# Loading filter rows in long transfers, and moving the reordering of columns into the moving read of the row-tiled matmuls

## The chip, the cores and the metric

One core of a Trainium2 chip. The metric is the device time of one execution in microseconds (us). Only runs of the fast state are compared; the slow ones are named. Ratios are computed as the mean time of one kernel's fast runs over the mean of the other kernel's fast runs of the same rounds, so they aren't quite the ratio of the medians that the text quotes. Intervals are at 95%.

Terms: PE is TensorE's matmuls and PEld its weight loads, DVE is VectorE, ACT is ScalarE, SP is SyncE, which issues most transfers. SBUF is the core's memory for data, PSUM the one that matmuls write. A matmul's stationary operand (the weights) is loaded first; then its moving operand is read (back to back, g1's matmuls of 128 columns start 56 ns apart, f2's of 256 columns 109 ns). An eviction copies a result from PSUM to SBUF. A row-tiled matmul here uses 64 of the 128 rows; two of them start 3 to 4 ns apart and run side by side.

## The reference, cut to what matters

```python
# x: (1, 2048, 512) bf16;  w_r, w_i: (2048, 257) bf16
def _A_ref(x, w_r, w_i):                       # spectral filter
    X = jnp.fft.rfft2(x.astype(jnp.float32), axes=(-2, -1))
    X = X * (w_r + 1j * w_i)
    return jnp.fft.irfft2(X, s=(S, D), axes=(-2, -1)).astype(jnp.bfloat16)

h  = x + _A_ref(_layernorm(x), w_r, w_i)
h2 = h + _B_ref(_layernorm(h), w1, b1, w2, b2) # MLP over the 2048 rows, F = 1376
```

The kernel computes both Fourier transforms as matmuls. Only the part around the product `X * W` matters here. The 257 columns of W are used as column 0 apart and 256 columns, which the transform delivers in two halves, by parity.

## The kernel before

The kernel builds a list of operations and orders them for each engine with a model of its own. These are the parts that the change touches (`...` marks cuts).

```python
add("W", [NP, NG, 2, LW], bf, rw)       # 128 x 32 rows g x (real, imaginary) x 257
add("CS", [NP, 16, 2, 2, NP], bf, rd)   # [group G][parity y][c][j]

# filter rows: three chunks (units 0, 1-3, 4-7), each row of 257 its own run of 514 B
for w, dram in ((0, A_w_r), (1, A_w_i)):
    for comp in range(2):
        d = W[comp::4, g0:g0 + ng, w, :]                     # "plus" rows, ascending
        lst.append(dma(..., d, bass.AP(dram.tensor, g0 * LW, [[64 * LW, 32], [LW, ng], [1, LW]]), ...))
        d = W[2 + comp::4, h0:h0 + nh, w, :]                 # "minus" rows, descending
        lst.append(dma(..., d, bass.AP(dram.tensor, (64 - h0) * LW, [[64 * LW, 32], [-LW, nh], [1, LW]]), ...))
        ...

# f2: matmuls into one bank, evicted to CS in the order (parity, c, j)
dst = CS[:, G, :, :, :].rearrange("p y c j -> p (y c j)")
cs_ops[G] = act(f"cs_{G}", dst, lambda bank: ps[:, bank, :], ACT.Copy, ...)

# x: row-tiled matmuls, 64 rows each, two at once, eight for each unit u
mm(f"x_{G}_{c}{r}", lambda bank, r=r, i=i: ps[:, bank + r, i * 256:i * 256 + 256],
   M[rows, ..., c, :], CS[rows, G, :, c, :], ...)

# V: product with the filter, VectorE, 2048 columns for each unit
wt = W[:, g0 + h * ng:g0 + h * ng + ng, :, :]
win = bass.AP(wt.tensor, wt.offset + 1, [list(wt.ap[0]), [LW, 2 * ng], [1, 2], [2, NP]])
eng.tensor_tensor(vout, s, win, ALU.mult)

# g1: V is the stationary operand
mm(f"g1_{g}_{par}{w}", ..., V[:, g, w, par * NP:par * NP + NP], R[:, ..., w, :], ...)
```

A unit u goes through f2 (TensorE), CS (ACT), x (TensorE), V (VectorE), g1 (TensorE), PQ (ACT). There are eight units. After all of them come g2 and g3, the second normalisation, and the MLP.

## Time and profile before

| | before |
|---|---|
| time | 134.44 us, median of 3 runs (134.16 to 134.53); a fourth run came later |
| V stage on VectorE | 22.0 to 39.9 us |
| first g2 matmul (all units done) | 41.32 us |
| row-tiled group of eight, start to the next group's start | 0.54 us |
| W's 514 B packets, first start to last end | 12.1 to 29.9 us |

The chain of waits by line, from the page of the kernel before. It follows the work back from the last instruction, each step to what released it.

```profile
PE ps L527 50%; DVE V L735 13%; DVE H L795 7%; DMA X<-in_A_x_dram 5%; ACT Y L545 5%; DVE TT L786 4%; DVE TT L788 4%; DVE HH L800 4%; ACT rs L545 1%; ACT FS L545 1%; DVE st L649 1%; SPq L517 1%; DVE OUT L825 1%; ACT PQ L545 0%; PE ps L617 0%
```

V holds 13% of it. No transfer but that of X is in it.

The timeline of VectorE around the V stage, kernel before. Columns: start in us, length in us, engine, line, operation, out<-in, shape, count, idle time before and what ended it.

```profile
22.02 17.88 DVE L735 TENSOR_TENSOR V<-ps,W 128x1024 bf16<-128x1024 f32 x10 [0.93 <-PE ps L527]
```

The ten V products run in one stretch without a gap between them.

The same view of TensorE, cut to the first and the last units. A line is a run of equal matmuls; `CS,EM` is a row-tiled group, `EM,V` is g1, `EM,Y` is f2, `EM,PQ` is g2.

```profile
21.27 0.61 PE L527 MATMUL ps<-CS,EM 64*128 64x256 bf16 x8
21.81 0.61 PE L527 MATMUL ps<-EM,Y 128*128 128x256 bf16 x4
...
34.66 0.61 PE L527 MATMUL ps<-CS,EM 64*128 64x256 bf16 x8
35.21 0.39 PE L527 MATMUL ps<-EM,Y 128*128 128x256 bf16 x2
35.44 0.72 PE L527 MATMUL ps<-EM,V 128*128 128x128 bf16 x10
36.29 0.61 PE L527 MATMUL ps<-CS,EM 64*128 64x256 bf16 x8
36.83 0.51 PE L527 MATMUL ps<-EM,V 128*128 128x128 bf16 x6
37.69 1.07 PE L527 MATMUL ps<-EM,V 128*128 128x128 bf16 x16 [0.35 <-DVE V L735]
38.91 0.61 PE L527 MATMUL ps<-EM,V 128*128 128x128 bf16 x8 [0.15 <-DVE V L735]
...
41.32 0.94 PE L527 MATMUL ps<-EM,PQ 128*128 128x256 bf16 x7 [0.69 <-ACT PQ L545]
```

Lengths overlap (a matmul of 256 columns takes about 270 ns, but the next starts about 109 ns after it), so read the starts: a row-tiled group takes 21.81 - 21.27 = 0.54 us. TensorE is nearly as full as VectorE here: busy 17.15 of the 17.90 us from 22.0 to 39.9.

The groups by form (busy us, mean ns of one | idle before), kernel before:

```profile
L735 DVE TENSOR_TENSOR V<-ps,W 128x2048 bf16<-128x2048 f32 x6 | 13.3, 2282 | 0.0
L527 PE MATMUL ps<-EM,V 128*128 128x128 bf16 x128 | 9.2, 219 | 0.5 <-DVE V L735 0.5
L545 ACT ACTIVATE CS<-ps 128x512 bf16<-128x512 f32 x15 | 8.3, 608 | 2.1 <-PE ps L527 2.1
L527 PEld LDWEIGHTS ps<-EM,V 128*128 128x128 bf16 x128 | 7.5, 98 | 2.3 <-issue 1.4 <-DVE V L735 0.8
L527 PE MATMUL ps<-CS,EM 64*128 64x256 bf16 x64 | 4.9, 272 | 0.2
L527 PE MATMUL ps<-EM,Y 128*128 128x256 bf16 x64 | 8.7, 273 | 0.4 <-ACT Y L545 0.4
L527 PE MATMUL ps<-EM,PQ 128*128 128x256 bf16 x64 | 9.0, 273 | 0.7 <-ACT PQ L545 0.7
```

And the transfers of the page, kernel before:

```profile
DMA packets 16648, 22.16 MB, mean 167 GB/s; under 512 B 2720, under 2 KB 12960, under 8 KB 16128
```

### The profile page before, as it was taken

The numbers are of one execution on the slowest core, as the hardware profiler recorded it, in microseconds if no ns is written. First come the engines' busy times: TensorE is split into PE (matmuls) and PEld (weight loads), VectorE is DVE, ScalarE is ACT, GpSimd is POOL, SyncE is SP. The second block draws the span as 40 slices with busy tenths as digits, with TensorE's granted clock in tenths as the row PEclk, the third lists the DMA queues.
The fourth block names the chain that finished last, engine by engine and source line by source line (L and its number), as shares of the span: only waits on it lengthen the run. The fifth ranks groups of instructions, "written<-read, shape, count | busy, mean of one in ns | idle before, by whom it ended". The sixth has DMA issues, their size and how long they took to land.

```text
span 133.0 us, 2023 instructions
## 1 busy us (share of the span) xinstructions
PE 125.4 (94%) x786; PEld 75.3 (57%) x786; DVE 69.2 (52%) x127; ACT 63.4 (48%) x146; POOL 12.2 (9%) x33
## 2 busy tenths in 40 slices
PE   6999989999987979999999999999999999999990
PEld 2356756878656726644434444456666666666660
DVE  0379975999990999999970000000242332423322
ACT  4569976878966999986679322222000000000000
POOL 0288830000300000000000000000000000000000
PEclk9999999999999999999999999999999999999999
DMA  3999698999999999992000000000111112111121
GB/s 94 335 370 382 178 276 229 304 317 264 411 430 430 398 411 409 419 281 89 0 0 0 0 0 0 5 0 0 39 39 64 55 39 81 42 59 59 39 79 39
DMA packets 16648, 22.16 MB, mean 167 GB/s; under 512 B 2720, under 2 KB 12960, under 8 KB 16128
## 3 DMA queue, kind: packets, MB, share of 16 engines
q1 hardware_dynamic: 16352, 21.52, 47.3%
q10 hardware_dynamic: 288, 0.52, 1.3%
q8 instruction: 6, 0.10, 0.3%
q14 instruction: 2, 0.02, 0.0%
HBM read 19.95 MB, written 2.10 MB: 166 GB/s over the span
## 4 chain that ended last, share of the span: by engine, by line
PE 51%; DVE 33%; ACT 8%; DMA 5%; issue 1%; SPq 1%; DVEq 0%; ACTq 0%
PE ps L527 50%; DVE V L735 13%; DVE H L795 7%; DMA X<-in_A_x_dram 5%; ACT Y L545 5%; DVE TT L786 4%; DVE TT L788 4%; DVE HH L800 4%; ACT rs L545 1%; ACT FS L545 1%; DVE st L649 1%; SPq L517 1%; DVE OUT L825 1%; ACT PQ L545 0%; PE ps L617 0%
## 5 line engine op out<-in xcount | busy, mean ns | idle before, releaser
L527 PE MATMUL ps<-HH,W 128*128 128x512 bf16 (+1 forms) x176 | 40.7, 379 | 1.2 <-DVE HH L800 0.9
L527 PE MATMUL ps<-GT,W 128*128 128x512 bf16 (+1 forms) x176 | 38.2, 379 | 0.0
L825 DVE SCALAR_TENSOR_TENSOR OUT<-ps,B2f,H 128x512 bf16<-128x512 f32 x16 | 12.0, 750 | 48.7 <-PE ps L527 48.7
L527 PEld LDWEIGHTS ps<-GT,W 128*128 128x128 bf16 (+1 forms) x176 | 25.4, 144 | 12.7
L527 PEld LDWEIGHTS ps<-HH,W 128*128 128x128 bf16 (+1 forms) x176 | 17.2, 100 | 21.2 <-DVE HH L800 1.9
L735 DVE TENSOR_TENSOR V<-ps,W 128x2048 bf16<-128x2048 f32 (+1 forms) x10 | 17.9, 1856 | 0.9 <-PE ps L527 0.9
L545 ACT ACTIVATE GT<-ps,B1f 128x512 bf16<-128x512 f32 (+1 forms) x11 | 7.1, 688 | 14.6 <-PE ps L527 14.6
L545 ACT ACTIVATE JK<-H,nm 128x512 bf16<-128x512 bf16 x16 | 11.6, 724 | 3.0 <-DVE H L795 2.9
L617 PE MATMUL ps<-ZT 128*128 128x512 bf16 x34 | 11.3, 479 | 1.3 <-DVE ZT L613 1.2
L649 DVE BATCH_NORM_STATS2 st<-X 128x6 f32<-128x512 bf16 x14 | 9.3, 668 | 5.3 <-DMA X<-in_A_x_dram 5.3
L795 DVE TENSOR_TENSOR H<-ps,TT 128x512 bf16<-128x512 f32 x16 | 10.9, 681 | 0.0
L545 ACT ACTIVATE PQ<-ps 128x512 bf16<-128x512 f32 x16 | 8.9, 603 | 3.5 <-PE ps L527 3.2
L545 ACT ACTIVATE EO<-ps 128x512 bf16<-128x512 f32 x16 | 9.3, 599 | 0.9 <-PE ps L527 0.9
L527 PE MATMUL ps<-EM,V 128*128 128x128 bf16 x128 | 9.2, 219 | 0.5 <-DVE V L735 0.5
L527 PE MATMUL ps<-EM,PQ 128*128 128x256 bf16 x64 | 9.0, 273 | 0.7 <-ACT PQ L545 0.7
L545 ACT ACTIVATE CS<-ps 128x512 bf16<-128x512 f32 x15 | 8.3, 608 | 2.1 <-PE ps L527 2.1
L527 PE MATMUL ps<-EM,Y 128*128 128x256 bf16 x64 | 8.7, 273 | 0.4 <-ACT Y L545 0.4
L527 PEld LDWEIGHTS ps<-EM,V 128*128 128x128 bf16 x128 | 7.5, 98 | 2.3 <-issue 1.4
L629 POOL TENSOR_SCALAR FS<-FP,rs 128x256 bf16<-128x256 bf16 x9 | 8.3, 935 | 1.3 <-ACT rs L545 1.3
L527 PE MATMUL ps<-FS,X 128*128 128x256 bf16 x64 | 8.3, 273 | 0.1
L786 DVE TENSOR_TENSOR TT<-ps,X 128x256 f32<-128x256 f32 x16 | 6.7, 416 | 3.3 <-PE ps L527 3.3
L527 PEld LDWEIGHTS ps<-EM,PQ 128*128 128x128 bf16 x64 | 6.2, 98 | 2.9 <-ACT PQ L545 0.9
(36 smaller groups left out, 80.3 us busy)
## 6 DMA issues: line engine op xcount, KB each, us to landing
W<-in_B_w_dram SPq DMA_DIRECT2D x4, 1376.0 KB, 11.0
W<-in_B_w_dram SPq DMA_DIRECT2D x10, 512.0 KB, 17.6
out_dram<-OUT SPq DMA_DIRECT2D x16, 128.0 KB, 1.7
W<-in_A_w_r_dram SPq DMA_DIRECT2D x4, 257.0 KB, 4.3
W<-in_A_w_i_dram SPq DMA_DIRECT2D x4, 257.0 KB, 5.0
X<-in_A_x_dram SPq DMA_DIRECT2D x4, 256.0 KB, 5.8
X<-in_A_x_dram SPq DMA_DIRECT2D x2, 512.0 KB, 7.7
W<-in_A_w_r_dram SPq DMA_DIRECT2D x4, 192.8 KB, 3.5
```

What stands on the lines that cost most here:

```text
L517: return eng.dma_start(dst, src)
L527: return K.op(name, "pe", lambda eng, bank: eng.matmul(outf(bank), lhsT, rhs, start=start, stop=stop), ins=ins or [lhsT, rhs], occ=occ, la ...
L545: return eng.activation(dst, s, func, **kw)
L617: return K.op(name, "pe", lambda eng, bank: eng.matmul(ps[:, bank, :], ZT[:, 0:NP], ZT[:, :], start=True, stop=True), ins=[ZT[:, :]], occ= ...
L629: dve(f"fs{i}", lambda eng, bank: eng.tensor_scalar(FS[:, i, :, :], FP[:, i, :, :], rs, None, op0=ALU.mult), [FP[:, i, :, :], rs], [FS[:, ...
L649: dve(f"st_{i}", lambda eng, bank, i=i, x=x: eng.bn_stats(ST[:, i, 0:6], x), [x], [ST[:, i, 0:6]], 512, prio=25)
L735: return eng.tensor_tensor(vout, s, win, ALU.mult)
L786: dve(f"tl_{s2}", lambda eng, bank, tt=tt, xl=xl: eng.tensor_tensor(tt[:, 0, :], ps[:, bank, 256:512], xl, ALU.add), [xl], [tt[:, 0, :]], ...
L788: dve(f"th_{s2}", lambda eng, bank, tt=tt, xh=xh: eng.tensor_tensor(tt[:, 1, :], xh, ps[:, bank, 256:512], ALU.subtract), [xh], [tt[:, 1, ...
L795: return eng.tensor_tensor(hs.rearrange("p (h d) -> p h d", h=2), e, tt[:, :, :], ALU.add)
L800: dve(f"hh_{s2}", lambda eng, bank, s2=s2, hs=hs: eng.tensor_scalar(HH[:, s2, :], hs, NM[:, s2:s2 + 1], R2[:, s2:s2 + 1], op0=ALU.add, op1 ...
L825: dve(f"fin{s2}", lambda eng, bank, dst=dst, bia=bia, hs=hs: eng.scalar_tensor_tensor(dst, ps[:, bank, :], bia, hs, op0=ALU.add, op1=ALU.add),
```

## The change

The intent is to make the filter's transfers cheaper. The plus rows ascend in memory, so with W laid out component first, `[NP, 2, NG, LW]`, the rows of one partition are one long run (2 to 8 KB instead of 514 B), and one transfer can write both component partitions. But then the V product's read of W would be a pattern of component, row, parity and column: four dimensions, where its operands in the trace have three (W's is 128 x 2 x 8 for a product of 2048 columns). Whether four would do was not tried. So the columns are put back in natural order before V: the row-tiled matmuls read CS alternately from both parities. V then reads W at unit stride, and g1 reads its weights in steps of two.

```diff
-    return 4 * (k2 * 2 + s) + 2 * sign + comp
+    return 4 * (k2 * 2 + s) + 2 * comp + sign
...
-    add("W", [NP, NG, 2, LW], bf, rw)
+    add("W", [NP, 2, NG, LW], bf, rw)
...
+            d = W[0:NP:2, w, g0:g0 + ng, :].rearrange("p g l -> p (g l)")
+            lst.append(dma(f"ld_wp{ch}_{w}", d, bass.AP(dram.tensor, g0 * LW, [[64 * LW, 32], [0, 2], [1, ng * LW]]), ...))
             for comp in range(2):
-                d = W[comp::4, g0:g0 + ng, w, :]
-                lst.append(dma(f"ld_wp{ch}_{w}{comp}", d, bass.AP(dram.tensor, g0 * LW, [[64 * LW, 32], [LW, ng], [1, LW]]), ...))
...              (minus rows: as before, other partitions; the loads of row 0 are joined too: 20 transfers, not 28)
-    M[rows, ...], CS[rows, G, :, c, :], ...
+    M[rows, ...], CS[rows, G, :, c, :].rearrange("p y j -> p j y"), ...
...
-    win = bass.AP(wt.tensor, wt.offset + 1, [list(wt.ap[0]), [LW, 2 * ng], [1, 2], [2, NP]])
+    win = bass.AP(wt.tensor, wt.offset + 1, [list(wt.ap[0]), [LW, ng], [NG * LW, 2], [1, 256]])
...
-    V[:, g, w, par * NP:par * NP + NP], R[...]
+    V[:, g, w, par::2], R[...]
```

More of the change, by code (lines that the diff above doesn't have):

```diff
@@ L578, in build_kernel @@
         for w, dram in ((0, A_w_r), (1, A_w_i)):
+            d = W[0:NP:2, w, g0:g0 + ng, :].rearrange("p g l -> p (g l)")
+            lst.append(dma(f"ld_wp{ch}_{w}", d, bass.AP(dram.tensor, g0 * LW, [[64 * LW, 32], [0, 2], [1, ng * LW]]),
+                           64 * ng * 514, prio=42 - ch, group=f"w{ch}"))
+            h0, nh = (g0, ng) if g0 else (1, ng - 1)
             for comp in range(2):
-                d = W[comp::4, g0:g0 + ng, w, :]
-                lst.append(dma(f"ld_wp{ch}_{w}{comp}", d, bass.AP(dram.tensor, g0 * LW, [[64 * LW, 32], [LW, ng], [1, LW]]),
-                               32 * ng * 514, prio=42 - ch, group=f"w{ch}", rate=300.0))
-                h0, nh = (g0, ng) if g0 else (1, ng - 1)
-                d = W[2 + comp::4, h0:h0 + nh, w, :]
+                d = W[1 + 2 * comp::4, w, h0:h0 + nh, :]
                 lst.append(dma(f"ld_wm{ch}_{w}{comp}", d, bass.AP(dram.tensor, (64 - h0) * LW, [[64 * LW, 32], [-LW, nh], [1, LW]]),
                                32 * nh * 514, prio=42 - ch, group=f"w{ch}", rate=300.0))
-                if g0 == 0:
-                    d = W[2 + comp::4, 0, w, :]
-                    lst.append(dma(f"ld_wz{ch}_{w}{comp}", d, bass.AP(dram.tensor, 32 * LW, [[64 * LW, 32], [1, LW]]),
-                                   32 * 514, prio=42 - ch, group=f"w{ch}", rate=300.0))
+            if g0 == 0:
+                d = W[1:NP:2, w, 0, :]
+                lst.append(dma(f"ld_wz{ch}_{w}", d, bass.AP(dram.tensor, 32 * LW, [[64 * LW, 32], [0, 2], [1, LW]]),
+                               64 * 514, prio=42 - ch, group=f"w{ch}", rate=300.0))
         for u in range(u0, u1):
@@ L721, in stage_x @@
                     mm(f"x_{G}_{c}{r}", lambda bank, r=r, i=i: ps[:, bank + r, i * 256:i * 256 + 256],
-                       M[rows, 1 if G == 0 and r == 0 else 0, c, :], CS[rows, G, :, c, :], unit, c == 0, c == 1, first, 13, 256, half=True, after=grp)
+                       M[rows, 1 if G == 0 and r == 0 else 0, c, :], CS[rows, G, :, c, :].rearrange("p y j -> p j y"), unit, c == 0, c == 1, first, 13, 256, half=True, after=grp)
                     first, grp = False, ()
@@ L727, in stage_x @@
         for h in range(nh):
-            wt = W[:, g0 + h * ng:g0 + h * ng + ng, :, :]
-            win = bass.AP(wt.tensor, wt.offset + 1, [list(wt.ap[0]), [LW, 2 * ng], [1, 2], [2, NP]])
+            wt = W[:, :, g0 + h * ng:g0 + h * ng + ng, :]
+            win = bass.AP(wt.tensor, wt.offset + 1, [list(wt.ap[0]), [LW, ng], [NG * LW, 2], [1, 256]])
             vout = V[:, g0 + h * ng:g0 + h * ng + ng, :, :].rearrange("p g w l -> p (g w l)")
@@ L751, in stage_g1 @@
                         lastg1[0] = mm(f"g1_{g}_{par}{w}", lambda bank, gi=gi, par=par: ps[:, bank, gi * 256 + par * 128:gi * 256 + par * 128 + 128],
-                           V[:, g, w, par * NP:par * NP + NP], R[:, 1 if g == 0 else 0, w, :], unit, w == 0, w == 1,
+                           V[:, g, w, par::2], R[:, 1 if g == 0 else 0, w, :], unit, w == 0, w == 1,
                            gi == 0 and par == 0 and w == 0 and not nw, 12, 128)
```

## The prediction

> **What bounds the kernel now.** The chain of waits: X lands (8 us), normalisation and ACT evictions of Y to 19.1 us, then VectorE: V products from 22.0 to 39.8 us without a gap (13% of the span), VectorE again from 43.2 to 68.5 us (H, TT, HH), then 61 us of matmuls. The filter W is never in that chain: the list of VectorE's waits shows no V product waiting for a transfer. The packet records have W's 8192 packets of 514 B running from about 12 to 30 us; the fifth V group, first user of the last chunk, starts at about 30.8 us. W1, queued behind, isn't needed before 48 us.
>
> **What the change does.**
> 1. DMA. The plus rows (4096 packets of 514 B, 28 ns each) become 384 long rows; 2 KB packets take 84 ns, 4 KB 159 ns. Estimate from those: 7.2 us of the 16 engines' time becomes about 5. 28 issues of about 0.62 us on SP become 20. W lands about 2 to 4 us sooner, W1 too. None of it is on the chain: worth 0.
> 2. V product. W is read at unit stride, not in steps of two. Each 2048-column product takes 2282 ns, the 1024-column one 1217, so 1.04 ns per column, the same slope as the unit-stride TT and H operations with f32 PSUM input (410 ns for 256, 681 for 512). I expect 2.28 us again: worth 0.
> 3. Row-tiled matmuls (64x256, 64 of them). The moving read now alternates between two places 256 B apart. Before, a group of eight takes 0.54 us from start to start (0.054 each, two at once, so 107 ns for 256 columns). [...] W2's loads with a 32-byte step take 144 ns against 98. My best estimate is twice the streaming time, +0.43 us per group.
> 4. g1's weights are read in steps of 4 B. [...] 98 ns may become 100 to 120, mostly hidden behind 56 ns starts (27 in 1.68 us).
>
> **How much is critical.** TensorE has little slack while V runs: the timeline of its instructions from 22 to 34 us shows group after group with about 0.1 us at each switch, and gaps of 0.1 to 0.5 us only after that. The row-tiled group of the seventh V ends at 35.27 us, just as that V starts; the fifth has 2.3 us of room, the sixth 0.9. Eight groups 0.43 us longer, minus the room, stretch the V stage by about 2.5 us. If strided reads are free, 0; if each column costs three or four times, 5 to 9.
>
> **Prediction.** 136.6 us, range 133.9 to 140.5. Faster by over 2%: 0.03; within 2%: 0.52; slower by over 2%: 0.45.
>
> **What would show each step.** W packets: about 4100 fewer of 514 B, W issued and landed earlier, and no wait in the chain shorter for it. V product: still 2.28 us. Row-tiled group of eight: start-to-start 0.9 to 1.0 us instead of 0.54, with VectorE now idle before V products, waiting for TensorE, some 2.5 us in sum. g1's weight loads near 98 ns, its starts near 56 ns. From the end of the V stage on, everything same but later.
>
> **What would make it wrong.** [...] The penalty may exceed two times, or strided weights may not hide behind 128-column matmuls: then 139 or more. The scheduler's order on TensorE is computed from modelled times, which the earlier modelled W could alter.

The transfers, the V product and g1's weights count 0, the row-tiled matmuls 8 x 0.43 = 3.4 us less 0.9 of room, about 2.5 us. With the 134.4 measured before that is 136.9; the text gives 136.6 and doesn't say where the 0.3 went. But the factor of two in step 3 stands as the author's estimate alone: the streaming time (8 x 0.054 = 0.43 us) is the trace's, its doubling is not. The same goes for the 100 to 120 ns of step 4.

One slip in this text and in some of the expectations: the two places that the row-tiled matmuls read are not 256 B apart. By the layout of CS, `[16, 2, 2, 128]` of 2-byte elements, the two parities lie 512 B apart.

## The result, and the profile after

138.43 us (138.37 to 138.50, 4 runs) against 134.49 us (134.16 to 134.55, 4 runs). The ratio is 1.0298, interval 1.0281 to 1.0316: slower by 3%. The prediction held 0.45 for slower by over 2% and 0.52 for within 2%, so the class that came was its second choice.

The chain of waits by line, after:

```profile
PE ps L527 60%; DVE H L795 7%; ACT Y L545 5%; DMA X<-in_A_x_dram 5%; DVE TT L786 4%; DVE TT L788 4%; DVE HH L800 4%; DVE V L735 3%; ACT rs L545 1%; ACT PQ L545 1%; ACT FS L545 1%; DVE st L649 1%; ACT CS L545 1%; SPq L517 1%; DVE OUT L825 1%
```

V fell from 13% to 3%, and TensorE's matmuls rose from 50% to 60%: in the V stage the chain now runs through TensorE. Two pieces of the chain in order of time (start, length), after:

```profile
37.83 1.19 PE ps L527 x8
...
39.04 3.44 DVE V L735 x2
```

The chain leaves TensorE behind the seventh row-tiled group, for the last V products. It doesn't pass through the eighth group, which starts at 39.99.

VectorE's timeline from 21 to 42 us, after:

```profile
22.53 6.75 DVE L735 TENSOR_TENSOR V<-ps,W 128x1024 bf16<-128x1024 f32 x4 [1.47 <-PE ps L527]
29.84 4.49 DVE L735 TENSOR_TENSOR V<-ps,W 128x2048 bf16<-128x2048 f32 x2 [0.56 <-PE ps L527]
35.41 2.29 DVE L735 TENSOR_TENSOR V<-ps,W 128x2048 bf16<-128x2048 f32 x1 [1.08 <-PE ps L527]
39.04 3.42 DVE L735 TENSOR_TENSOR V<-ps,W 128x2048 bf16<-128x2048 f32 x2 [1.34 <-PE ps L527]
```

The products now wait four times for TensorE, 4.4 us in sum against 0.9 before.

TensorE's timeline, the same places, after:

```profile
21.25 1.14 PE L527 MATMUL ps<-CS,EM 64*128 64x256 bf16 x8
22.32 0.61 PE L527 MATMUL ps<-EM,Y 128*128 128x256 bf16 x4
...
37.83 1.14 PE L527 MATMUL ps<-CS,EM 64*128 64x256 bf16 x8
38.91 0.39 PE L527 MATMUL ps<-EM,Y 128*128 128x256 bf16 x2
39.14 0.72 PE L527 MATMUL ps<-EM,V 128*128 128x128 bf16 x10
39.99 1.14 PE L527 MATMUL ps<-CS,EM 64*128 64x256 bf16 x8
41.06 1.40 PE L527 MATMUL ps<-EM,V 128*128 128x128 bf16 x22
42.61 0.61 PE L527 MATMUL ps<-EM,V 128*128 128x128 bf16 x8
...
45.02 1.16 PE L527 MATMUL ps<-EM,PQ 128*128 128x256 bf16 x9 [0.69 <-ACT PQ L545]
```

A row-tiled group takes 22.32 - 21.25 = 1.07 us instead of 0.54. The last group shows where a part is given back: from its start to the g1 line of eight that follows takes 38.91 - 36.29 = 2.62 us before and 42.61 - 39.99 = 2.62 us after, because TensorE had been waiting there for V anyway. So seven groups count: 7 x 0.53 = 3.7 us. The first g2 matmul starts at 45.02 instead of 41.32, 3.70 us later, and what follows is the same work later, but for the stretch behind the last OUT instruction, 2.2 us instead of 2.5.

The span from the first to the last instruction therefore grew by 3.5 us only (136.4 to 136.6 against 133.0). The rest of the 3.9 us lies outside it, where no profile looks: time less span is 1.90 to 1.97 us in the runs of the changed kernel. This follows the transfers: all five kernels with the new ones have 1.90 to 1.99 us there, the kernel before and all eight with the old ones 1.47 to 1.60. What takes these 0.4 us stays open.

The groups by form, after:

```profile
L735 DVE TENSOR_TENSOR V<-ps,W 128x2048 bf16<-128x2048 f32 x6 | 13.6, 2286 | 3.0 <-PE ps L527 3.0
L527 PE MATMUL ps<-CS,EM 64*128 64x256 bf16 x64 | 9.1, 404 | 0.2
L527 PE MATMUL ps<-EM,V 128*128 128x128 bf16 x128 | 9.0, 220 | 0.1
L545 ACT ACTIVATE CS<-ps 128x512 bf16<-128x512 f32 x15 | 8.3, 608 | 3.7 <-PE ps L527 3.7
L527 PEld LDWEIGHTS ps<-EM,V 128*128 128x128 bf16 x128 | 7.6, 98 | 3.0 <-issue 2.7 <-DVE V L735 0.3
```

Only the row-tiled matmul changed, 272 to 404 ns. V at unit stride takes what it took (2286 ns), and g1's weights in steps of 4 B still load in 98 ns.

The transfers, after:

```profile
DMA packets 12808, 22.16 MB, mean 162 GB/s; under 512 B 2592, under 2 KB 8736, under 8 KB 12160
```

The packet records show the intended gain: 8192 packets of 514 B became 4096, plus 128 each of 2056, 6168 and 8224 B. An 8224 B packet takes 316 ns (median) where 514 B take 28, so 26 against 18 bytes per ns. W's packets took 15.7 us of the 16 engines' time before and 13.2 us after. The last 514 B packet of W ended at 26.2 us instead of 29.9, and the loads of W1, which wait for it, were issued from 26.8 us instead of 30.5. No engine's wait list names either as what a computation waited for.

### The profile page after: what moved, and what is told of

The parts are those of the page before. It is cut to its first block, busy times and chain, and to the rows that moved or that the text cites. A ratio compares the mean times of both kernels' runs of the same rounds, so it can differ in the third digit from the quotient of the medians.

```text
span 136.4 us, 2005 instructions
## 1 busy us (share of the span) xinstructions
PE 128.6 (94%) x776; PEld 75.2 (55%) x786; DVE 69.4 (51%) x127; ACT 63.3 (46%) x146; POOL 12.2 (9%) x33
## 4 chain that ended last, share of the span: by engine, by line
PE 60%; DVE 23%; ACT 9%; DMA 5%; issue 1%; SPq 1%; ACTq 0%
PE ps L527 60%; DVE H L795 7%; ACT Y L545 5%; DMA X<-in_A_x_dram 5%; DVE TT L786 4%; DVE TT L788 4%; DVE HH L800 4%; DVE V L735 3%; ACT rs L545 1%; ACT PQ L545 1%; ACT FS L545 1%; DVE st L649 1%; ACT CS L545 1%; SPq L517 1%; DVE OUT L825 1%
## 5 line engine op out<-in xcount | busy, mean ns | idle before, releaser
L617 PE MATMUL ps<-ZT 128*128 128x512 bf16 x32 | 10.6, 472 | 1.6 <-DVE ZT L613 1.2
L527 PE MATMUL ps<-CS,EM 64*128 64x256 bf16 x64 | 9.1, 404 | 0.2
```

The source lines that it names most:

```text
L527: return K.op(name, "pe", lambda eng, bank: eng.matmul(outf(bank), lhsT, rhs, start=start, stop=stop), ins=ins or [lhsT, rhs], occ=occ, la ...
L617: return K.op(name, "pe", lambda eng, bank: eng.matmul(ps[:, bank, :], ZT[:, 0:NP], ZT[:, :], start=True, stop=True), ins=[ZT[:, :]], occ= ...
```

## The experiments

Theory A: the alternating moving read alone costs the time, through TensorE. Theory B: the new transfers disturb the engines, since W and W1 now arrive earlier. Theory C: g1's weights in steps of two cost it. Except where said, results are correct. In all experiments but the two with split products, the order of instructions on TensorE is that of the kernel before.

### stride_only: the new arithmetic on the old transfers

```diff
-    M[rows, ...], CS[rows, G, :, c, :]                                  # kernel before
+    M[rows, ...], CS[rows, G, :, c, :].rearrange("p y j -> p j y")
-    [[LW, 2 * ng], [1, 2], [2, NP]]     # W
+    [[LW, 2 * ng], [1, 256]]
-    V[:, g, w, par * NP:par * NP + NP]
+    V[:, g, w, par::2]
```

> The kernel before with its 28 old transfers and old layout of W, but with the arithmetic of the change: alternating moving read of the row-tiled matmuls, W read at unit stride, g1's weights read in steps of two. Theory A (the alternating moving read alone costs the time): 138.4 us, the same as the changed kernel; a row-tiled group of eight takes 1.07 us from start to start. Theory B (the new transfers, which put W and W1 into SBUF earlier, disturb the engines): 134.5 us, groups of 0.54 us. Theory C (g1's weights in steps of 4 B): 138.4 us too, so this run doesn't part A from C.

Measured: 138.22 us (138.09 to 138.36) against 134.49; ratio 1.0277 (1.0263 to 1.0291). Groups by form, this run:

```profile
L527 PE MATMUL ps<-CS,EM 64*128 64x256 bf16 x64 | 9.1, 403 | 0.2
```

The loss is there without the new transfers, so B falls as its cause. (The changed kernel's 0.2 us more is the 0.4 us outside the span, less 0.2 us inside it.)

### cs_natural: the reordering moved into the evictions

```diff
-    add("CS", [NP, 16, 2, 2, NP], bf, rd)                               # changed kernel
+    add("CS", [NP, 16, 2, NP, 2], bf, rd)
-    dst = CS[:, G, :, :, :].rearrange("p y c j -> p (y c j)")
+    dst = CS[:, G, :, :, :].rearrange("p c j y -> p y (c j)")           # the eviction's source is cut in y to match
-    CS[rows, G, :, c, :].rearrange("p y j -> p j y")
+    CS[rows, G, c, :, :].rearrange("p j y -> p (j y)")                  # contiguous
```

> The changed kernel with one thing undone: the evictions of CS write the columns in natural order (step of two in SBUF), so that the moving read of the row-tiled matmuls is contiguous again. New transfers, unit-stride W and g1's weights in steps of two stay. Theory A: 134.5 us (within 0.3), groups of eight at 0.54 us again, moving matmul 272 ns, CS evictions still near 608 ns. Theories B and C: 138.4 us still. If writing CS in steps of two slows ACT, its evictions exceed 608 ns and the time lies between.

Measured: 134.88 us (134.83 to 135.22, 5 runs) against 134.49; ratio 1.0036 (1.0023 to 1.0049). Groups by form, this run:

```profile
L545 ACT ACTIVATE CS<-ps 128x512 bf16<-128x512 f32 x15 | 10.3, 755 | 1.6 <-PE ps L527 1.5
L527 PE MATMUL ps<-CS,EM 64*128 64x256 bf16 x64 | 4.9, 272 | 0.6 <-ACT CS L545 0.6
```

With the new transfers, unit-stride W and stepped g1 weights all kept, the loss is gone but for 0.4 us. C falls. Here I had expected one thing wrongly: an eviction that writes in steps of 4 B takes 755 ns, not 608, and the row-tiled matmuls now wait 0.6 us for ACT in sum. In the trace the stretch from the first row-tiled group to the first g2 matmul is 0.4 us longer than before (20.46 against 20.05). But the evictions aren't all of the difference: the spans of the five runs average 133.0 us, as the kernel before's do, and the 0.4 us that the new transfers add outside the span are in the time too. step4b_b below has the slow evictions on the old transfers and loses about 0.5 us, all of it inside the span.

### stride_first4 and stride_last4: the alternating read in half of the units

As stride_only, but each of its three edits only for `u < 4`, or only for `u >= 4`.

> Old transfers; alternating moving read (with natural order of V) only in the first four of the eight units. Theory A, worked out from the lists of TensorE's groups: each of four groups 0.53 us longer makes TensorE 2.1 us late at the fifth unit; before the sixth and seventh V there is almost no room (0.9 and 0 us), TensorE's own gaps of 0.1 to 0.3 us give some back: 134.5 + about 1.7, that is 136.2 us (135.7 to 136.6). If any strided group sets off a fixed loss elsewhere (order, bank release), not near half of 3.9.

> As the run before, but in the last four units only. Theory A: 4 x 0.53 = 2.1 us, less the room of the fifth unit (2.3 us, which swallows its own delay but hands it on to the sixth), gaps after 33 us of 0.2 + 0.3 + 0.5 us: about +1.3, that is 135.8 us (135.3 to 136.4). First four and last four together should make about the 3.9 us of all eight or a little less, since each half can use room that the whole uses once.

Measured: first four 136.59 us (136.34 to 136.69), last four 136.08 us (136.00 to 136.20), against 134.49; ratios 1.0153 (1.0139 to 1.0167) and 1.0118 (1.0103 to 1.0134), both under 2% and both clear of 1. That is 2.1 and 1.6 us more. Four groups at 0.53 are 2.1; with the last group free, three are 1.6. My expected values (1.7 and 1.3) were low, because they gave TensorE credit for the room before V and for its short gaps. There was no such credit except at the last group.

### f2_psum_b: the reordering moved into f2's PSUM write

The first submissions of four kernels (f2_psum, step4b, block2, g2_alt) reached no chip; the same kernels were sent again under labels with `_b`.

```diff
-    ps[:, bank, par * 256:par * 256 + 256]     # f2's output, changed kernel
+    ps[:, bank, par::2]                        # steps of 8 B; eviction and moving read contiguous
```

> The changed kernel with the reordering moved once more: the f2 matmuls write their columns into PSUM in steps of two (8 bytes), the CS evictions are contiguous on both sides, the moving read of the row-tiled matmuls is contiguous. If writing PSUM with a step costs TensorE nothing: f2 matmuls 273 ns, CS evictions 608 ns, groups of eight 0.54 us, 134.5 us. If it slows the matmul as alternating reads do, f2 takes about 400 ns (64 matmuls, +0.13 us each, a good half of them in the V stage): 138 to 141 us. [...] I expect the slow case at 0.6.

Measured: 140.92 us (140.83 to 141.06) against 134.38; ratio 1.0486 (1.0465 to 1.0507). Groups by form, this run:

```profile
L527 PE MATMUL ps<-EM,Y 128*128 128x256 bf16 x64 | 15.3, 416 | 0.4 <-ACT Y L545 0.4
L527 PE MATMUL ps<-CS,EM 64*128 64x256 bf16 x64 | 4.9, 272 | 0.1
```

The cost moved to f2: 416 ns instead of 273. It is dearer there because more of it is paid: the f2 matmuls run one after the other, and their starts went from 109 to 216 ns apart, for 64 of them an estimated 6.8 us. The row-tiled ones run in 32 pairs, 0.13 us more each, 4.3 us.

### step4b_b, step8b and step16b: regular steps

The figures are estimates: 272 ns for step4b_b, 275 to 300 ns for step8b (from block2_b's 298, which ran before it), 404 ns for step16b (the alternating read's).

```diff
-    CS[rows, G, :, c, :]                                                # kernel before, CS in natural order
+    CS[rows, G, c, :, :].rearrange("p j y -> p y j")                    # step4b_b: 4 B, correct result
+    ... .rearrange("p (m s) -> p s m", s=4)                             # step8b: 8 B, wrong on purpose
+    ... .rearrange("p (m s) -> p s m", s=8)                             # step16b: 16 B, wrong on purpose
```

> The kernel before, with CS written in natural order by the evictions and read by the row-tiled matmuls in steps of two elements (4 bytes), so that everything after is as before. [...] moving matmul 272 ns, groups 0.54 us, time as the run with natural CS, 134.9. Step theory (any read whose inner step isn't one element is slow): 404 ns, groups 1.07 us, 138.3 us or more.

> Wrong result on purpose: as the run before in steps of four elements (8 bytes), 64 in a row[...]. [...] by the run with blocks of two (298 ns): 275 to 300 ns a matmul, groups 0.56 to 0.66 us, time 135.0 to 135.7 us.

> Wrong result on purpose: the kernel before with natural CS (755 ns evictions), the moving read in steps of eight elements (16 bytes), 32 in a row, eight passes: [...] no jumps back and forth. [...] as the alternating read, 404 ns a matmul and groups of 1.07 us, time near 138.5 to 139. If only alternating between far places costs[...]: 272 ns, 135.0 us as the run with steps of 4 bytes.

Measured, in this order: 134.99, 138.02 and 146.62 us against 134.38, 134.42 and 134.42; ratios 1.0037 (1.0012 to 1.0062), 1.0263 (1.0237 to 1.0289) and 1.0924 (1.0870 to 1.0978). Groups by form, one fence for each run, same order:

```profile
L545 ACT ACTIVATE CS<-ps 128x512 bf16<-128x512 f32 x15 | 10.3, 754 | 1.7 <-PE ps L527 1.5
L527 PE MATMUL ps<-CS,EM 64*128 64x256 bf16 x64 | 5.0, 274 | 0.6 <-ACT CS L545 0.6
```

```profile
L527 PE MATMUL ps<-CS,EM 64*128 64x256 bf16 x64 | 8.5, 397 | 0.6 <-ACT CS L545 0.6
```

```profile
L527 PE MATMUL ps<-CS,EM 64*128 64x256 bf16 x64 | 15.7, 621 | 0.6 <-ACT CS L545 0.6
```

Steps of 4 B are nearly free (274 ns against 272), so the step theory falls. Steps of 8 B cost nearly as much as the alternating read (397 ns against 404), where I had estimated 275 to 300. Steps of 16 B cost more than twice as much as the alternating read (349 ns more against 132), where I had estimated the same. In the 16-byte run the granted clock was also 0.977 to 0.988, so its time holds a small part that isn't the read's own. The 621 ns are not touched by it: the trace has a clock of 1.00 up to 45 us, behind seven of the eight groups.

### block2_b: two neighbours from each place

```diff
-    CS[rows, G, :, c, :].rearrange("p y j -> p j y")                    # changed kernel
+    CS[rows, G, :, c, :].rearrange("p y (b j) -> p b y j", j=2)         # wrong on purpose
```

Of the figures expected here, the first (272 ns) is a read as fast as a contiguous one, the second (338 ns) half of the alternating read's extra time.

> Wrong result on purpose: the changed kernel, but the moving read takes two neighbouring elements from one place, then two from the other, 256 B apart, instead of one each. [...] 272 ns, groups 0.54 us, 134.5 us. [...] half the extra, about 338 ns a matmul, groups 0.80 us, near 136.3 us. Loop theory (each restart of a short inner loop costs): also half, since there are as many inner loops of two as before, or no gain at all, 404 ns.

Measured: 135.24 us (135.06 to 135.39) against 134.38; ratio 1.0062 (1.0041 to 1.0083). Groups by form:

```profile
L527 PE MATMUL ps<-CS,EM 64*128 64x256 bf16 x64 | 5.7, 298 | 0.2
```

Half as many jumps cost one fifth of the extra time (26 of 132 ns). A fixed price for each jump would have halved it. A fixed price for each restart of the inner loop of two, of which both reads have equally many, would have left it whole. Neither fits.

### g2_alt_b: an alternating read in full-array matmuls

```diff
-    D2[:, par, pq, :]                                                   # moving read of g2, kernel before
+    D2[:, par, pq, :].rearrange("p (h m) -> p m h", h=2)                # wrong on purpose
```

> Wrong result on purpose: the kernel before, its row-tiled matmuls contiguous, but the moving read of D2 in the full-array matmuls g2 (128 rows, 256 columns) alternates between places 256 B apart. If the cost belongs to the read itself: g2's matmul goes from 273 to about 404 ns, as in the row-tiled ones. If it comes from two row tiles reading at once, it stays at 273 or grows less. Time of the kernel: g2 runs beside a VectorE-bound stage with spare TensorE time filled by mm1, 64 x 0.13 = 8 us more TensorE work in 25 us, which pushes mm1 later: between 134.5 and 142 us.

Measured: 141.89 us (141.76 to 142.31) against 134.38; ratio 1.0563 (1.0536 to 1.0589). Groups by form:

```profile
L527 PE MATMUL ps<-EM,PQ 128*128 128x256 bf16 x64 | 17.6, 406 | 0.7 <-ACT PQ L545 0.7
```

406 ns (the granted clock of this run was 0.984), about the 404 of the row-tiled matmuls, though the two places are 256 B apart here and 512 B there. So the cost belongs to the read; row tiling neither causes it nor hides it.

### split_new and split_old: what the transfers are worth by themselves

Column order and moving read as before; each V product is two of 1024 columns, one for each component. split_new has the new transfers and layout, split_old the old ones.

```diff
-    nh = 2 if u in V_SPLIT else 1
-    ng = 4 // nh
+    nh = 2                      # h is now the component
+    ng = 4
-    [LW, 2 * ng], [1, 2], [2, NP]       # old layout; the changed kernel has [LW, ng], [NG * LW, 2], [1, 256]
+    [2 * LW, ng], [1, 2], [2, NP]       # split_old; split_new has [LW, ng], [1, 2], [2, NP]
```

> The new transfers and the new layout of W, without the alternating read: the order of columns is as before, and each V product is two of 1024 columns (one for each component of W)[...]. Correct result. Isolates the worth of the transfers, beside the next run, which has the same products on the old transfers. If the transfers are worth nothing (my theory): the same as the next run within 0.2 us. If W and W1 arriving earlier helps or disturbs: apart by more than 0.3 us. The split itself should cost 1.1 us a product instead of 2.2 for both, some 0.05 us a unit: 134.9 us (134.5 to 135.6).

> The kernel before with only the V products split by component into two of 1024 columns. 134.9 us (134.5 to 135.6), equal to the run with the new transfers within 0.2 us if the transfers are off the critical path.

Measured: split_new 1.0195 (1.0172 to 1.0218), split_old 1.0184 (1.0158 to 1.0210); medians of the fast runs 137.10 and 136.98 us against 134.42. The interval of each ratio lies on both sides of 2%, so each is slower, but by over 2% or under stays unclear. One of split_new's six runs took 262.8 us, with matmuls about half as fast throughout (679 ns each in the MLP instead of 379) at a recorded clock of 1.00, and two of split_old's took 139.5 and 139.7 us at a granted clock of 0.972; all three are left out. VectorE, TensorE and ACT have the same instructions in the same order in both, and the times are the same within about 0.1 us: the transfers are worth nothing here. This is a sum of two parts: split_new's spans are 0.3 us shorter (135.1 to 135.2 against 135.3 to 135.6), and 0.4 us more lie outside them. (split_new's only trace is that of the 262.8 us run, so the waits below are split_old's.)

That both lost 2.6 us I hadn't expected. The product itself takes 1219 ns, as expected. The schedule on TensorE came out in another order, V waits 1.9 us for TensorE instead of 0.9, and the last unit's g1 can no longer start on half of its rows, since both halves need both components. How the 2.6 us divide between these wasn't tested. As a way to keep the long rows, the split loses to the natural-order eviction.

## Why the prediction was right, and where a term was off

- **The transfers are worth nothing: right.** 4096 fewer packets of 514 B (about 4100 predicted), W done 3.7 us sooner (2 to 4), W1 issued sooner, and no wait on the chain shortened. split_new against split_old shows it without the other edits. That 0.4 us more would appear outside the span was not foreseen; here the shorter spans nearly pay for it.
- **The V product gains nothing from unit stride: right.** 2282 before, 2286 ns after.
- **g1's stepped weights stay near 98 ns and hidden: right.** 98 ns, and cs_natural, which keeps them, is slower than the kernel before by only 0.4 us in all, for which other causes are at hand. W2's loads in the MLP, in steps of 32 B, take 144 ns in both kernels.
- **The alternating read slows the row-tiled matmuls and TensorE turns into the limit: right in mechanism.** stride_only shows the loss with nothing but the arithmetic changed, cs_natural shows it gone, the two halves show that it adds up by groups.
- **The size was low in two terms.** Predicted: twice the streaming time, +0.43 us a group. Measured: +0.53 us (1.07 against 0.54), about 2.2 times. The factor of two was a guess that no trace backed, so that it came near is luck. And "minus the room, stretch the V stage by about 2.5 us": eight groups of 0.43 are 3.4, from which I took 0.9 for room. Measured: 3.70 us, that is 8 x 0.53 = 4.2 less 0.5. The room was counted at the wrong place: the prediction itself says that the seventh group ended just as its V started, so by its own figures V was late by seven times 0.43, 3.0 us, and the sixth unit's 0.9 couldn't be taken off. I compared each group's end with the start of its V product. But TensorE was itself a continuous chain up to the last row-tiled group; most of its short gaps were waits for CS evictions, which follow f2 matmuls on the same engine and so move along with it. Only behind the last group, where it waited for V, was there a gap to fill. stride_last4 (three groups' worth) and stride_first4 (four) confirm this.
- **The reason given for the slow read was not shown.** It came from no trace; W2's 144 ns against 98, which the text sets beside it, are weight loads, not a moving read. It gave the right sign for the alternating read, and 272 ns for step4b_b came near (274), but the other figures that I drew from it failed: 275 to 300 ns for step8b, which took 397, and 404 for step16b, which took 621. What the runs show, from the start of one group to the next instruction's start: contiguous 0.54 us, 4 B 0.56, two from each place 0.65, 8 B 1.00, alternating 1.07, 16 B 1.90. In the trace's records, the four pairs of a group start 109, 114, 137, 227, 243 and 451 ns apart (medians, same order). So from 4 to 8 to 16 B, twice the step takes twice the time; a contiguous read, in steps of 2 B, takes about what 4 B take. That doesn't cover the alternating read, which jumps 512 B each time and costs about as much as steps of 8 B. What gives all of these stays open.

No version beat the kernel before. The V stage is bound by VectorE (17.9 us without a gap) and at the same time by TensorE (busy 17.15 of these 17.90 us), and no transfer is in its way.

## What to carry to other kernels

Before you speed up a transfer, look whether anything waits for it; here a quarter of the packets went and no wait became shorter, while the price was paid on the fullest engine. What a reordering costs depended on where it was done: in this kernel the moving read cost 3.7 us, the matmul's PSUM write 6.5 us, the eviction's write about 0.5 us, and the old step of two in the VectorE product nothing (2282 ns against 2286 at unit stride). When two engines are both full in a stage, room that you read off against one of them isn't room: look for the place where the engine you load really waits for the other. And compare the time with the span: what a change adds outside the span shows in no profile.
